# A new step order for a fused chunk-attention and phase-mixing kernel

## The chip, the cores and the metric

One Trainium2 chip, one core. The metric is the device time of one execution in microseconds; a kernel's time is the median over several runs.

## The reference

Attention inside chunks of 64 positions, then a token-mixing layer with phases, and a channel mixing with a relu. Eight batches, eight heads of 64 (so 512 channels), 576 positions, all in float32.

```python
# attention, for each batch, head and chunk of 64 positions
scores = (1 / sqrt(64)) * q_c @ k_c.T
attn = softmax(scores)                 # over the 64 keys of the chunk
x = attn @ v_c                         # heads side by side: [8, 576, 512]
# mixing
theta = x @ w_theta                    # 512 x 512
zr, zi = x * cos(theta), x * sin(theta)
y = w_tok_r @ zr + w_tok_i @ zi        # over the 576 positions
u = x + y
out = u + relu(u @ w_ch)               # 512 x 512
```

## The kernel before

**Tiles.** Two batches make a pair; there are four pairs, p = 0 to 3. A pair's 1152 positions are nine tiles of 128: tiles 0 to 3 are the first batch's, 5 to 8 the second's, and tile 4 holds the last 64 positions of each. For the attention part the tiles are taken in five groups: A (tiles 0, 1), B (2, 3), M (tile 4 alone), C (5, 6), D (7, 8). Everything is computed in fp16 with fp32 sums.

**Steps.** The whole kernel is a list of steps, written out in the string `ORDER`. A step is `kind.pg` or `kind.pg.slot`: the kind, the pair, the group or tile, and for steps that write PSUM the slot. There are three wide slots (two banks each) and two thin ones (one bank each); a step that writes a slot waits until the step that last used it has been read. The kinds are:

- on GpSimd (POOL), loads: `q`, `k`, `v` (two DMAs of 128 KB for a group, of 64 KB for M; L174, L182), `lw` the token weights in four parts (L192, L197), `lc` the channel weights (L200); `init` makes the identity matrix with a memset and a select on POOL.
- on TensorE (PE): `T` transposes q and k of a group (L262), `S` the scores (L308), `V0` and `V1` attention times v for the heads of either half (L341), `X` transposes x (L372), `H` (or `Ha`, `Hb` for a single tile) theta (L410), `Y` (or `Ya`, `Yb`, `Yc` in three parts) token mixing of one tile, 9 matmuls of 512 columns (18 narrower ones for tile 4; L480), `U` transposes u (L497), `W` channel mixing, 4 matmuls (L517), `TW` transposes the token weights (L236), `D` an idle matmul on a blank tile (L157).
- on VectorE (DVE): `tq` copies a T result from PSUM to SBUF (L285, L287), `v0` and `v1` divide by the softmax sum (L353, L354), `xv` copies an X result (L384), `z`, `za`, `zb` multiply x by cos and sin (L440 to L449), `y` adds x (L488), `uv` copies a U result (L511), `w` adds the relu and u (L526), `twd` copies a TW result (L247, L249).
- on ScalarE (ACT): `tqa`, `x` and `ua` do what `tq`, `xv` and `uv` do, `e` is the exponential (L321), `g`, `ga`, `gb` the cosine and sine (L426, L430[...]), `ct` casts w_theta once, `sa` issues half of a late tile's store.
- on SyncE (SP), in one queue: `Ud` and `Xd` transpose u or x of late tiles by DMA (L505, L393), `zm` moves half of the middle tile's z between partitions (L454, L455), `st` issues a tile's store, two DMAs, one for the last pair (L543), `lt` loads w_theta once.
- `new` only hands out a pair's tiles.

Each engine runs its own steps strictly in the order of the list; between engines, semaphores make a step wait for what it reads and for the buffers that it writes. A step late on one engine holds back all that stands behind it there.

**Buffers.** q and k of a group lie together in one of eight `qk` buffers, taken in turn at the group's first load, and given back by `T`. v has room for two pairs. x, zr and zi of a pair lie in one of two sets.

The string is read once, in this loop:

```python
with tc.manual_schedule():
    for step in ORDER:
        kind, at, *slot = step.split(".")
        g = int(at[1]) if at[1].isdigit() else at[1]
        work[kind](int(at[0]), g, *map(int, slot))
```

Of the kernel before, what the change touches and what calls it, by code (L numbers as in the profile page):

```python
# [15 lines left out]


ORDER = """
ones.00 D.00.0 lt.00 D.00.1 D.00.0 D.00.1 D.00.0 D.00.1 q.0M q.0B D.00.0 D.00.1 D.00.0
new.00 D.00.1 D.00.0 D.00.1 D.00.0 lw.00 D.00.1 q.0A D.00.0 D.00.1 k.0M lw.01 D.00.0  # L20
D.00.1 D.00.0 D.00.1 D.00.0 init.00 k.0B D.00.1 D.00.0 D.00.1 D.00.0 D.00.1 D.00.0
D.00.1 k.0A D.00.0 D.00.1 D.00.0 D.00.1 D.00.0 ct.00 D.00.1 D.00.0 D.00.1 TW.00.0 D.00.0
v.0M v.0A q.0C D.00.1 D.00.0 D.00.1 D.00.0 D.00.1 T.0M.1 tq.0M S.0M.2 e.0M TW.01.1
D.00.0 T.0B.2 twd.00 D.00.1 D.00.0 v.0B D.00.1 T.0A.0 D.00.0 q.0D lw.02 twd.01 D.00.1
V0.0M.1 tq.0A tqa.0B v0.0M S.0A.2 e.0A V1.0M.0 S.0B.1 v1.0M D.00.0 e.0B X.0M.2 V0.0A.0
k.0C V1.0A.1 x.0M H.0M.2 new.10 v0.0A v1.0A X.0A.0 xv.0A V1.0B.1 Ha.0A.1 v1.0B V0.0B.0
g.0M ga.0A v0.0B lw.03 k.0D z.0M Hb.0A.0 v.0C q.1C X.0B.1 TW.02.2 twd.02 gb.0A T.0C.0
x.0B q.1D Ha.0B.1 zm.0M Hb.0B.0 tq.0C zb.0A za.0A v.0D TW.03.1 ga.0B gb.0B S.0C.2 twd.03
q.1M T.0D.0 e.0C lc.00 Ya.02.1 zb.0B Ya.03.0 k.1D Yb.02 Yb.03 za.0B Yc.03 y.03 Yc.02
y.02 Ya.01.0 Yb.01 U.02.1 tqa.0D V1.0C.1 S.0D.2 q.1B e.0D V0.0C.0 Yc.01 ua.02 V1.0D.2  # L30
v1.0C v0.0C X.0C.1 V0.0D.0 Ya.00.1 y.01 Yb.00 k.1M xv.0C H.0C.1 Yc.00 v0.0D v1.0D y.00
v.1M X.0D.0 xv.0D T.1D.2 k.1C v.1D tq.1D g.0C U.03.0 U.00.1 k.1B ua.00 uv.03 H.0D.0
W.03.1 q.1A z.0C U.01.0 T.1M.1 g.0D w.03 st.03 S.1D.2 W.02.1 tq.1M S.1M.0 T.1C.1 ua.01
z.0D e.1D Y.06.0 w.02 tq.1C e.1M V0.1M.2 S.1C.1 T.1B.0 v.1C q.2C q.2M k.1A q.2D v0.1M
y.06 W.01.1 e.1C V1.1M.2 tq.1B V1.1D.1 v1.1M v.1B Y.04.0 q.3B w.01 V0.1C.0 st.02 v1.1D
S.1B.2 V0.1D.1 v0.1D k.2M e.1B Y.08.1 y.04 Y.07.0 v.1A k.2C X.1M.2 x.1M v0.1C T.1A.1
X.1D.0 V1.1C.2 y.08 U.04.1 ua.04 y.07 v1.1C st.01 tq.1A x.1D Y.05.0 V0.1B.2 X.1C.0
S.1A.1 e.1A x.1C y.05 W.04.1 U.06.0 v0.1B w.04 H.1M.2 W.00.1 q.2A uv.06 w.00 g.1M
V1.1B.1 v1.1B H.1C.0 z.1M H.1D.2 g.1C U.08.0 U.05.1 uv.08 V0.1A.1 V1.1A.0 v1.1A ua.05
v0.1A W.08.0 W.06.1 g.1D w.06 v.2M k.2D w.08 st.04 T.2C.0 st.00 z.1D X.1B.1 q.2B X.1A.2  # L40
x.1B v.2D W.05.1 x.1A H.1B.1 H.1A.2 v.2C w.05 tq.2C U.07.0 k.2A zm.1M g.1B z.1C Y.16.1
S.2C.0 st.06 v.2B ua.07 g.1A y.16 T.2D.1 T.2M.2 tq.2D new.20 k.2B U.16.0 Y.18.1 tq.2M
q.3D e.2C ua.16 y.18 z.1B S.2M.1 e.2M z.1A st.05 S.2D.0 T.2A.2 V0.2M.1 Y.15.0 y.15
tqa.2A W.16.1 e.2D V0.2C.2 v0.2M v0.2C v.3D V1.2C.0 k.3B q.3A w.16 v1.2C Y.13.0 S.2A.1
V1.2D.2 v.2A V0.2D.0 W.07.1 y.13 e.2A w.07 v1.2D v0.2D st.08 Y.10.0 U.15.1 st.16 V1.2M.1
v1.2M y.10 X.2C.2 T.2B.0 ua.15 Y.14.1 tq.2B q.3M x.2C X.2M.1 y.14 S.2B.2 X.2D.0 x.2M
e.2B Y.17.0 U.10.1 V0.2B.1 k.3A T.3A.2 v.3A v0.2B x.2D ua.10 q.3C T.3B.0 y.17 tqa.3B
W.15.1 w.15 k.3M H.2M.1 W.10.0 U.13.1 tq.3A uv.13 st.07 w.10 g.2M H.2C.0 V1.2B.2 V1.2A.1
st.10 g.2C W.13.1 U.18.0 ua.18 k.3D st.15 v1.2B z.2M w.13 st.13 H.2D.2 Y.12.0 g.2D
W.18.1 v1.2A T.3D.0 y.12 S.3B.1 z.2C T.3M.2 zm.2M k.3C w.18 z.2D Y.11.0 tq.3M v.3M e.3B  # L50
Y.27.1 S.3M.1 tqa.3D T.3C.2 y.11 S.3A.0 e.3M st.18 V0.2A.1 Y.28.0 tq.3C y.27 v0.2A e.3A
V0.3M.0 Xd.2A Ud.11 new.30 S.3D.2 v.3B V0.3B.1 e.3D v0.3M Ud.14 y.28 Xd.2B v0.3B v.3C
Y.25.1 V1.3M.0 V1.3A.2 S.3C.1 Ud.17 v1.3M Ud.27 Y.26.0 y.25 V0.3A.0 v1.3A e.3C V1.3C.1
v0.3A Xd.3A V1.3B.2 v1.3C W.14.1 w.14 y.26 H.2A.0 Xd.3M v1.3B W.11.1 H.2B.1 w.11 st.14
st.11 g.2A z.2A g.2B Ud.12 W.27.0 w.27 st.27 Ud.26 H.3A.2 g.3A W.17.1 Ud.25 z.2B w.17
st.17 H.3M.0 g.3M Xd.3B Y.24.0 y.24 V1.3D.1 Ud.24 V0.3D.2 V0.3C.0 v0.3D W.12.1 Ud.28
v1.3D w.12 Y.21.0 Y.22.1 st.12 v0.3C Xd.3D y.21 W.26.0 Ud.21 y.22 w.26 W.25.1 w.25
Y.23.0 y.23 st.26 st.25 H.3B.2 z.3A W.24.1 w.24 W.21.0 w.21 Xd.3C st.21 Ud.23 z.3M zm.3M
W.28.1 H.3D.1 Y.20.0 w.28 st.24 Ud.22 st.28 y.20 H.3C.0 g.3B z.3B W.23.1 g.3D w.23
Y.31.0 Y.32.1 y.31 W.22.0 st.23 g.3C Ud.20 z.3C y.32 Ud.31 w.22 Ud.32 Y.30.1 z.3D W.20.0  # L60
y.30 Y.38.1 w.20 st.20 y.38 st.22 W.31.0 Ud.38 w.31 Ud.30 Y.37.1 y.37 Y.35.0 y.35 W.32.1
w.32 W.38.0 Ud.35 sa.31 w.38 Y.33.1 W.30.0 y.33 st.38 sa.38 st.32 st.31 Y.36.1 sa.32
w.30 Y.34.0 y.36 sa.30 st.30 y.34 Ud.37 W.35.1 w.35 sa.35 Ud.33 W.33.0 w.33 sa.33 W.37.1
Ud.36 Ud.34 w.37 W.36.0 st.35 w.36 st.33 W.34.1 D.00.0 sa.37 st.37 D.00.0 D.00.0 st.36
w.34 D.00.1 D.00.0 sa.36 D.00.1 D.00.0 D.00.1 D.00.0 sa.34 D.00.1 D.00.0 st.34
""".split()


# [565 lines left out]
```

The softmax here doesn't subtract the row's maximum and nothing guards it: scores larger than these inputs give would overflow.

## Time and profile before

| | us |
|---|---|
| median of 9 runs (lowest to highest) | 203.41 (202.08 to 205.58) |
| the profiled execution, whole | 202.6 |
| the profiled execution, span from first to last instruction | 200.8 |
| PE busy, of it idle matmuls | 190.8, 17.1 |
| DVE, ACT, POOL busy | 127.8, 93.0, 106.1 |
| PE clock granted, over the span | 1.0 |
| last load issued by POOL, from the span's start | 115.3 |

All times inside the kernel are counted from the start of the span. The profile is of one execution, 0.8 us below the median. Busy time says how full an engine is, not what it waits for: the chain of work that ended last tells which engine or transfer set the time in a stretch, and a timeline gives each group of instructions with its start, its length, and in brackets the idle time before it and what ended that.

| stretch (us) | PE busy in it | idle matmuls in it | POOL |
|---|---|---|---|
| 0 to 11.7 | nearly all | 36 | loads from 1.24 on |
| 11.7 to 36.0 | work from the first transpose to tile 02's mixing | 13 | loads |
| 36.0 to 69.1 | all but 1.0 us | 0 | loads |
| 69.1 to 137 | all | 0 | loads until 115.3 |
| 137 to 196.1 | all but 2.0 us | 0 | idle |
| 196.1 to 200.8 | last store | 11 | idle |

### The profile page before, as it was taken

What the parts mean: (1) busy time and instruction counts of PE and PEld (TensorE: products, weight loads), DVE (VectorE), ACT (ScalarE), POOL (GpSimd) and SP (SyncE); (2) the same over time, 40 slices, a digit from 0 to 9 for tenths busy, and PEclk for the clock granted to TensorE, in tenths of its full rate; (3) what the DMA queues carried; (4) which work ended last, traced back from release to release, by engine and by line L of the source; (5) the groups of instructions that cost most, each with busy time, mean ns of one, the idle gap of its engine ahead of it and who ended that gap; (6) DMA issues with size and microseconds to landing.
All of it is one profiled execution on the core that took longest, in us unless ns stands there. A gap on an engine that the chain in (4) does not pass through costs nothing.

```text
span 200.8 us, 6347 instructions
## 1 busy us (share of the span) xinstructions
PE 190.8 (95%) x2766; PEld 95.1 (47%) x2766; DVE 127.8 (64%) x235; ACT 93.0 (46%) x100; POOL 106.1 (53%) x133
## 2 busy tenths in 40 slices
PE   7988789999999999999999999999999899999986
PEld 2434455545554645455465555543444344344432
DVE  0014689387885867948874786977684566844461
ACT  2304877556922488797247976427900444000000
POOL 7999999788998999987998800000000000000000
PEclk9999999999999999999999999999999999999999
DMA  5999999999999999999999992179777886683775
GB/s 191 170 169 155 159 186 167 153 176 145 168 191 186 155 166 213 180 207 170 163 208 153 144 229 64 32 145 117 152 123 148 176 168 131 134 171 64 216 167 163
DMA packets 140090, 32.01 MB, mean 159 GB/s; under 512 B 132768, under 2 KB 134944, under 8 KB 140064
## 3 DMA queue, kind: packets, MB, share of 16 engines
q0 software_dynamic: 114288, 16.02, 119.0%
q1 hardware_dynamic: 25056, 14.43, 31.2%
q10 hardware_dynamic: 720, 1.18, 2.0%
q8 instruction: 21, 0.34, 0.7%
q14 instruction: 5, 0.04, 0.1%
HBM read 33.06 MB, written 9.44 MB: 212 GB/s over the span
## 4 chain that ended last, share of the span: by engine, by line
PE 57%; DMA 21%; POOL 18%; issue 3%; DVE 0%; SPq 0%; POOLq 0%
PE ps_y L480 25%; PE ps_uw L517 12%; POOL qk L174 11%; PE ps_theta L410 10%; DMA v<-in_v_dram 7%; DMA uT<-u 5%; POOL v L182 5%; DMA qk<-in_q_dram 4%; DMA wch<-in_moe_w_ch_dram 3%; PE ps_qkT L262 2%; PE ps_x L341 2%; PE ps_sT L308 2%; DMA xT<-x 2%; POOL wnat L192 1%; PE ps_idle L157 1%
## 5 line engine op out<-in xcount | busy, mean ns | idle before, releaser
L480 PEld LDWEIGHTS <-wT 128*128 128x128 f16 (+1 forms) x360 | 30.8, 100 | 35.0 <-issue 1.2
L480 PE MATMUL ps_y<-zr,wT 128*128 128x512 f16 (+1 forms) x180 | 44.4, 381 | 0.0
L480 PE MATMUL ps_y<-zi,wT 128*128 128x512 f16 (+1 forms) x180 | 41.8, 379 | 0.0
L488 DVE TENSOR_TENSOR u<-ps_y,x 128x512 f16<-128x512 f32 x36 | 24.7, 687 | 24.8 <-PE ps_y L480 23.3
L517 PE MATMUL ps_uw<-wch,uT 128*128 128x512 f16 x144 | 36.4, 380 | 1.7 <-DMA uT<-u 1.7
L182 POOL DMA_DIRECT2D v<-in_v_dram x40 | 34.0, 870 | 3.4 <-DMA qk<-in_q_dram 1.1
L174 POOL DMA_DIRECT2D qk<-in_q_dram x40 | 34.1, 874 | 2.7 <-issue 1.0
L174 POOL DMA_DIRECT2D qk<-in_k_dram x40 | 34.2, 868 | 2.4 <-DMA v<-in_v_dram 0.8
L410 PE MATMUL ps_theta<-wtheta,xT 128*128 128x512 f16 x144 | 34.3, 380 | 0.5 <-DMA xT<-x 0.3
L426 ACT ACTIVATE cos<-ps_theta,pihalf 128x1024 f16<-128x1024 f32 (+1 forms) x22 | 21.1, 960 | 26.0 <-PE ps_theta L410 23.1
L321 ACT ACTIVATE eT<-ps_sT 128x1024 f16<-128x1024 f32 (+1 forms) x20 | 18.6, 938 | 28.2 <-PE ps_sT L308 28.2
L526 DVE SCALAR_TENSOR_TENSOR o<-ps_uw,u 128x512 f32<-128x512 f32 x36 | 24.7, 688 | 10.5 <-PE ps_uw L517 9.8
L354 DVE TENSOR_TENSOR x<-ps_x,recip 128x512 f16<-128x512 f32 (+1 forms) x40 | 25.5, 638 | 1.4
L517 PEld LDWEIGHTS <-uT 128*128 128x128 f16 x144 | 12.7, 97 | 18.5 <-DMA uT<-u 4.6
L410 PEld LDWEIGHTS <-xT 128*128 128x128 f16 x144 | 13.2, 98 | 16.4 <-DMA xT<-x 0.8
L430 ACT ACTIVATE sin<-ps_theta 128x1024 f16<-128x1024 f32 (+1 forms) x22 | 19.0, 864 | 0.0
L157 PE MATMUL ps_idle<-blank 128*128 128x512 f16 x60 | 17.1, 432 | 1.3 <-DVE pihalf L145 1.2
L287 DVE COPY qkT<-ps_qkT 128x2048 f16<-128x2048 f16 x11 | 13.4, 1216 | 4.5 <-PE ps_qkT L262 4.5
L353 DVE RECIPROCAL recip<-ps_x 128x8 f32<-128x8 f32 (+1 forms) x40 | 7.8, 196 | 10.6 <-PE ps_x L341 10.3
L341 PE MATMUL ps_x<-v,eT 64*64 64x65 f16 x576 | 11.9, 196 | 2.0 <-DMA v<-in_v_dram 1.6
L262 PE MATMUL ps_qkT<-id,qk 64*128 64x64 f16 x576 | 12.2, 191 | 1.2 <-DMA qk<-in_k_dram 1.2
L341 PEld LDWEIGHTS <-eT 64*64 64x64 f16 x576 | 8.2, 106 | 9.2 <-issue 5.1
(42 smaller groups left out, 137.9 us busy)
## 6 DMA issues: line engine op xcount, KB each, us to landing
out_dram<-o SPq DMA_DIRECT2D x63, 128.0 KB, 2.8
qk<-in_q_dram POOLq DMA_DIRECT2D x32, 128.0 KB, 6.6
qk<-in_k_dram POOLq DMA_DIRECT2D x32, 128.0 KB, 6.7
v<-in_v_dram POOLq DMA_DIRECT2D x32, 128.0 KB, 6.5
out_dram<-o ACTq DMA_DIRECT2D x9, 128.0 KB, 2.8
theta<-in_moe_w_theta_dram SPq DMA_DIRECT2D x1, 1024.0 KB, 5.6
wnat<-in_moe_w_tok_r_dram POOLq DMA_DIRECT2D x2, 288.0 KB, 6.1
wnat<-in_moe_w_tok_i_dram POOLq DMA_DIRECT2D x2, 288.0 KB, 6.4
```

Source lines behind the costliest of these rows:

```text
L157: nc.tensor.matmul(ps, blank[:, 0:P], blank, start=True, stop=True)
L174: nc.gpsimd.dma_start(nats[p, g][rows, which, r], (q, k)[which][b, :, t0 : t0 + n, :].rearrange("h s d -> s h d"),)
L182: nc.gpsimd.dma_start(v16[rows, slot + r, :, 0:D], v[b, :, t0 : t0 + n, :].rearrange("h s d -> s h d"),)
L341: nc.tensor.matmul(psv[half[r], to, h4, :], eT[rows, h % 2, r if n == 2 else 0, h // 2, :], v16[rows, slot + (r if n == 2 else 0), h, 0 : ...
L354: nc.vector.tensor_tensor(out=st[p]["x"][:, j0 : j0 + n, f * NE * D : (f + 1) * NE * D].rearrange("p c (h d) -> p c h d", h=NE), in0=psv[: ...
L410: nc.tensor.matmul(ps[:, j * DM : j * DM + DM], xT[:, (j + (t or 0)) * NDB + db, :], wtheta16[:, db, :], start=(db == 0), stop=(db == NDB ...
L426: nc.scalar.activation(out=cos[:, 0:n].rearrange("p a e -> p (a e)"), in_=pin, func=AF.Sin, bias=pihalf, scale=1.0,)
L430: nc.scalar.activation(out=sin[:, 0:n].rearrange("p a e -> p (a e)"), in_=pin, func=AF.Sin)
L480: nc.tensor.matmul(ps[rows], wT[:, kt, cols], z[:, jz, :], start=(kt == 0), stop=(kt == 2 * KT),)
L488: nc.vector.tensor_tensor(out=u, in0=st[p].pop(("ps_y", j))[:, 0:DM], in1=st[p]["x"][:, j], op=ALU.add)
L517: nc.tensor.matmul(ps, uT[:, db * P : db * P + P], wch16[:, db, :], start=(db == 0), stop=(db == NDB - 1),)
L526: nc.vector.scalar_tensor_tensor(out=o, in0=st[p].pop(("ps_uw", j)), scalar=0.0, in1=u, op0=ALU.max, op1=ALU.add)
```

## The change

Only the string `ORDER` changes. The 651 steps are permuted; every tile goes through the same computation with the same matmuls, loads and stores. Twenty-five copies out of PSUM change the engine (`tq` and `tqa`, `x` and `xv`, `ua` and `uv`), most PSUM slots are given anew, and idle matmuls are put in other places. Loads change places in POOL's queue, and the transposes and stores in SP's.

The old order's head and end, and the whole new order:

```diff
-ones.00 D.00.0 lt.00 D.00.1 D.00.0 D.00.1 D.00.0 D.00.1 q.0M q.0B D.00.0 D.00.1 D.00.0
-new.00 D.00.1 D.00.0 D.00.1 D.00.0 lw.00 D.00.1 q.0A D.00.0 D.00.1 k.0M lw.01 D.00.0
-D.00.1 D.00.0 D.00.1 D.00.0 init.00 k.0B D.00.1 D.00.0 D.00.1 D.00.0 D.00.1 D.00.0
-D.00.1 k.0A D.00.0 D.00.1 D.00.0 D.00.1 D.00.0 ct.00 D.00.1 D.00.0 D.00.1 TW.00.0 D.00.0
-v.0M v.0A q.0C D.00.1 D.00.0 D.00.1 D.00.0 D.00.1 T.0M.1 tq.0M S.0M.2 e.0M TW.01.1
-D.00.0 T.0B.2 twd.00 D.00.1 D.00.0 v.0B D.00.1 T.0A.0 D.00.0 q.0D lw.02 twd.01 D.00.1
-V0.0M.1 tq.0A tqa.0B v0.0M S.0A.2 e.0A V1.0M.0 S.0B.1 v1.0M D.00.0 e.0B X.0M.2 V0.0A.0
-k.0C V1.0A.1 x.0M H.0M.2 new.10 v0.0A v1.0A X.0A.0 xv.0A V1.0B.1 Ha.0A.1 v1.0B V0.0B.0
-g.0M ga.0A v0.0B lw.03 k.0D z.0M Hb.0A.0 v.0C q.1C X.0B.1 TW.02.2 twd.02 gb.0A T.0C.0
-x.0B q.1D Ha.0B.1 zm.0M Hb.0B.0 tq.0C zb.0A za.0A v.0D TW.03.1 ga.0B gb.0B S.0C.2 twd.03
-q.1M T.0D.0 e.0C lc.00 Ya.02.1 zb.0B Ya.03.0 k.1D Yb.02 Yb.03 za.0B Yc.03 y.03 Yc.02
-y.02 Ya.01.0 Yb.01 U.02.1 tqa.0D V1.0C.1 S.0D.2 q.1B e.0D V0.0C.0 Yc.01 ua.02 V1.0D.2
-v1.0C v0.0C X.0C.1 V0.0D.0 Ya.00.1 y.01 Yb.00 k.1M xv.0C H.0C.1 Yc.00 v0.0D v1.0D y.00
-v.1M X.0D.0 xv.0D T.1D.2 k.1C v.1D tq.1D g.0C U.03.0 U.00.1 k.1B ua.00 uv.03 H.0D.0
-W.03.1 q.1A z.0C U.01.0 T.1M.1 g.0D w.03 st.03 S.1D.2 W.02.1 tq.1M S.1M.0 T.1C.1 ua.01
-z.0D e.1D Y.06.0 w.02 tq.1C e.1M V0.1M.2 S.1C.1 T.1B.0 v.1C q.2C q.2M k.1A q.2D v0.1M
-y.06 W.01.1 e.1C V1.1M.2 tq.1B V1.1D.1 v1.1M v.1B Y.04.0 q.3B w.01 V0.1C.0 st.02 v1.1D
...
-st.11 g.2A z.2A g.2B Ud.12 W.27.0 w.27 st.27 Ud.26 H.3A.2 g.3A W.17.1 Ud.25 z.2B w.17
-st.17 H.3M.0 g.3M Xd.3B Y.24.0 y.24 V1.3D.1 Ud.24 V0.3D.2 V0.3C.0 v0.3D W.12.1 Ud.28
-v1.3D w.12 Y.21.0 Y.22.1 st.12 v0.3C Xd.3D y.21 W.26.0 Ud.21 y.22 w.26 W.25.1 w.25
-Y.23.0 y.23 st.26 st.25 H.3B.2 z.3A W.24.1 w.24 W.21.0 w.21 Xd.3C st.21 Ud.23 z.3M zm.3M
-W.28.1 H.3D.1 Y.20.0 w.28 st.24 Ud.22 st.28 y.20 H.3C.0 g.3B z.3B W.23.1 g.3D w.23
-Y.31.0 Y.32.1 y.31 W.22.0 st.23 g.3C Ud.20 z.3C y.32 Ud.31 w.22 Ud.32 Y.30.1 z.3D W.20.0
-y.30 Y.38.1 w.20 st.20 y.38 st.22 W.31.0 Ud.38 w.31 Ud.30 Y.37.1 y.37 Y.35.0 y.35 W.32.1
-w.32 W.38.0 Ud.35 sa.31 w.38 Y.33.1 W.30.0 y.33 st.38 sa.38 st.32 st.31 Y.36.1 sa.32
-w.30 Y.34.0 y.36 sa.30 st.30 y.34 Ud.37 W.35.1 w.35 sa.35 Ud.33 W.33.0 w.33 sa.33 W.37.1
-Ud.36 Ud.34 w.37 W.36.0 st.35 w.36 st.33 W.34.1 D.00.0 sa.37 st.37 D.00.0 D.00.0 st.36
-w.34 D.00.1 D.00.0 sa.36 D.00.1 D.00.0 D.00.1 D.00.0 sa.34 D.00.1 D.00.0 st.34
+ones.00 D.00.0 lt.00 D.00.1 D.00.0 D.00.1 D.00.0 q.0M D.00.1 D.00.0 D.00.1 q.0B D.00.0
+D.00.1 lw.00 D.00.0 D.00.1 D.00.0 D.00.1 D.00.0 D.00.1 init.00 D.00.0 D.00.1 D.00.0
+D.00.1 D.00.0 D.00.1 D.00.0 D.00.1 q.0A D.00.0 D.00.1 D.00.0 D.00.1 TW.00.0 D.00.0
+D.00.1 twd.00 D.00.0 D.00.1 D.00.0 ct.00 k.0M D.00.1 T.0M.1 lw.01 k.0B tq.0M D.00.0
+D.00.1 D.00.0 S.0M.2 e.0M v.0M TW.01.0 D.00.1 D.00.0 T.0B.1 D.00.1 D.00.0 D.00.1 k.0A
+v.0A tqa.0B new.00 D.00.0 q.0D twd.01 T.0A.0 V1.0M.2 S.0B.1 D.00.1 D.00.0 v.0B D.00.1
+D.00.0 tqa.0A q.0C V0.0M.0 e.0B v1.0M lw.02 S.0A.2 D.00.1 v0.0M e.0A X.0M.1 V1.0A.0
+v1.0A x.0M lw.03 k.0D V0.0A.2 D.00.0 v0.0A k.0C H.0M.1 X.0A.0 V0.0B.2 q.1M xv.0A v0.0B
+g.0M Ha.0A.1 Hb.0A.0 V1.0B.0 v.0C gb.0A ga.0A z.0M TW.02.1 q.1D v1.0B twd.02 X.0B.2
+xv.0B lc.00 TW.03.0 zb.0A za.0A Hb.0B.0 gb.0B Ha.0B.1 ga.0B twd.03 T.0C.1 tq.0C v.0D
+q.1C Ya.02.0 Yb.02 Ya.03.1 Yb.03 za.0B zm.0M S.0C.2 e.0C q.1B k.1D zb.0B T.0D.0 tq.0D
+k.1M Yc.03 Yc.02 y.03 V1.0C.1 V0.0C.0 y.02 Ya.01.1 Yb.01 v.1M U.03.0 ua.03 v1.0C Yc.01
+v.1D k.1C y.01 W.03.0 w.03 S.0D.2 Ya.00.1 v0.0C e.0D U.02.0 X.0C.1 V1.0D.0 xv.0C v1.0D
+V0.0D.2 v0.0D Yb.00 Yc.00 q.1A k.1B H.0C.1 q.2C y.00 q.2M uv.02 k.1A X.0D.0 st.03 xv.0D
+T.1D.2 U.01.1 v.1C v.1A tq.1D g.0C H.0D.0 q.3C uv.01 g.0D z.0C T.1M.2 W.01.0 w.01 st.01
+W.02.1 v.1B T.1C.1 q.2A S.1D.0 tqa.1M z.0D S.1M.2 Y.06.0 w.02 U.00.1 e.1D k.2M V0.1D.0
+tq.1C T.1B.1 e.1M tqa.1B y.06 new.10 V1.1D.2 Y.04.0 V0.1M.1 v0.1D V1.1M.0 v1.1D ua.00
+q.2D S.1C.2 v1.1M q.3M q.3A y.04 Y.08.1 k.2C v0.1M U.04.0 y.08 uv.04 e.1C X.1M.0 X.1D.2
+x.1M T.1A.1 V0.1C.0 Y.07.1 tqa.1A xv.1D U.08.0 v0.1C V1.1C.2 uv.08 S.1A.0 v1.1C e.1A
+q.2B S.1B.1 W.04.0 y.07 H.1M.2 U.06.1 w.04 e.1B W.08.0 st.02 uv.06 Y.05.1 k.3A w.08 g.1M
+X.1C.0 V0.1B.1 V1.1B.2 y.05 U.07.0 v0.1B x.1C W.00.1 w.00 k.2A z.1M ua.07 H.1D.0 v1.1B
+U.05.0 g.1D uv.05 H.1C.1 g.1C new.20 V1.1A.2 V0.1A.0 k.2D W.06.1 v0.1A W.05.0 X.1B.0
+v1.1A X.1A.1 w.06 v.2M st.04 xv.1A w.05 x.1B v.2C k.2B T.2C.2 W.07.1 z.1C st.08 tqa.2C
+st.00 H.1B.1 w.07 z.1D H.1A.0 zm.1M Y.16.0 g.1B y.16 v.2D T.2M.2 z.1B S.2C.1 g.1A T.2D.0
+st.05 tqa.2M U.16.1 ua.16 Y.18.0 Y.15.1 e.2C tq.2D S.2D.2 y.18 S.2M.0 z.1A V1.2C.1
+W.16.0 y.15 U.15.1 st.07 v1.2C e.2D w.16 V0.2C.2 uv.15 T.2A.1 v.2B e.2M V1.2M.0 U.18.0
+v1.2M Y.13.1 T.2B.0 ua.18 v.3M tq.2A v0.2C tqa.2B V0.2M.1 q.3D y.13 X.2C.2 q.3B Y.10.0
+xv.2C S.2B.2 v0.2M V1.2D.1 v.2A k.3B S.2A.0 st.06 Y.14.1 e.2B V0.2D.2 e.2A v1.2D st.16
+y.10 V0.2B.1 X.2M.0 v0.2D x.2M W.18.0 y.14 H.2M.0 v0.2B Y.17.1 w.18 U.10.0 uv.10 g.2M
+H.2C.2 y.17 z.2M st.18 U.13.0 Y.12.1 ua.13 V1.2B.1 v1.2B T.3B.0 g.2C T.3A.2 zm.2M tqa.3B
+y.12 X.2D.1 k.3M v.3B xv.2D W.13.0 H.2D.1 z.2C W.10.1 T.3M.0 w.13 tqa.3A w.10 g.2D v.3A
+V1.2A.2 W.15.0 Y.11.1 v1.2A V0.2A.1 S.3B.2 z.2D w.15 st.15 st.13 y.11 k.3D st.10 Ud.17
+Ud.14 v0.2A tqa.3M T.3D.0 e.3B Y.25.0 tq.3D Ud.12 S.3A.1 Ud.11 k.3C T.3C.0 V0.3B.2 y.25
+tq.3C e.3A new.30 v0.3B Xd.2B Y.28.1 V1.3B.1 y.28 V0.3A.0 v0.3A S.3C.2 e.3C Y.27.0 v1.3B
+y.27 S.3M.0 V1.3A.2 e.3M S.3D.1 v.3C W.17.1 W.12.0 V0.3M.0 v1.3A Xd.2A Ud.27 Xd.3A e.3D
+V0.3C.2 V1.3M.1 w.17 v1.3M W.14.1 st.17 w.12 H.2B.1 g.2B v0.3C v0.3M W.11.0 w.11 H.2A.2
+Ud.28 W.27.0 w.14 Y.26.1 st.12 H.3A.0 st.11 Xd.3B g.2A Ud.25 st.14 w.27 z.2B g.3A st.27
+z.2A Xd.3M Y.24.0 v.3D y.26 V1.3D.1 y.24 V1.3C.2 V0.3D.0 Y.22.1 v1.3C y.22 W.28.0 Ud.24
+Ud.22 w.28 W.25.1 st.28 v0.3D H.3M.2 Xd.3C g.3M z.3A Y.20.0 Ud.26 w.25 y.20 Ud.20 v1.3D
+Y.23.1 H.3B.0 g.3B W.26.0 st.25 z.3M zm.3M y.23 w.26 st.26 W.24.1 Xd.3D w.24 W.20.0 w.20
+W.22.1 H.3C.2 z.3B st.24 Y.32.0 w.22 Y.21.1 st.22 st.20 g.3C Ud.23 y.32 Y.30.0 z.3C
+Ud.32 y.30 H.3D.1 g.3D y.21 Y.31.0 y.31 W.23.1 w.23 Ud.30 W.30.0 w.30 Ud.21 Ud.31 st.30
+Y.33.1 W.32.0 st.23 z.3D y.33 W.31.1 w.32 w.31 Y.38.0 st.31 Y.35.1 sa.30 sa.32 y.38
+Ud.38 st.32 y.35 Ud.35 W.21.0 w.21 sa.31 Y.37.1 y.37 W.38.0 Y.36.1 w.38 st.21 Ud.33
+Y.34.0 y.36 W.35.1 st.38 Ud.37 Ud.36 sa.38 y.34 W.37.0 w.35 w.37 Ud.34 W.33.1 w.33 st.35
+st.37 W.36.0 w.36 W.34.1 D.00.0 D.00.0 sa.35 sa.33 st.33 w.34 D.00.1 D.00.0 sa.36 D.00.1
+D.00.0 sa.37 D.00.1 D.00.0 st.36 D.00.1 st.34 D.00.0 sa.34 D.00.1
```

More of the change, by code (lines that the diff above doesn't have):

```diff
@@ L31 @@
-v1.0C v0.0C X.0C.1 V0.0D.0 Ya.00.1 y.01 Yb.00 k.1M xv.0C H.0C.1 Yc.00 v0.0D v1.0D y.00
-v.1M X.0D.0 xv.0D T.1D.2 k.1C v.1D tq.1D g.0C U.03.0 U.00.1 k.1B ua.00 uv.03 H.0D.0
-W.03.1 q.1A z.0C U.01.0 T.1M.1 g.0D w.03 st.03 S.1D.2 W.02.1 tq.1M S.1M.0 T.1C.1 ua.01
-z.0D e.1D Y.06.0 w.02 tq.1C e.1M V0.1M.2 S.1C.1 T.1B.0 v.1C q.2C q.2M k.1A q.2D v0.1M
-y.06 W.01.1 e.1C V1.1M.2 tq.1B V1.1D.1 v1.1M v.1B Y.04.0 q.3B w.01 V0.1C.0 st.02 v1.1D
-S.1B.2 V0.1D.1 v0.1D k.2M e.1B Y.08.1 y.04 Y.07.0 v.1A k.2C X.1M.2 x.1M v0.1C T.1A.1
@@ L37 @@
[L37 to L54, printed above, removed]
```

## The prediction

> **What bounds the kernel now.** I read the page's busy row first, then the chain that ended last, then the timelines of PE, ACT, DVE and SP.
>
> ```profile
> span 200.8 us, 6347 instructions
> PE 190.8 (95%) x2766; PEld 95.1 (47%) x2766; DVE 127.8 (64%) x235; ACT 93.0 (46%) x100; POOL 106.1 (53%) x133
> ```
>
> PE is busy 95% of the span, but 17.1 us of its 190.8 are the 60 idle matmuls (L157), so some 174 us are work. The rest of the span is where an order can gain: a head until work flows, gaps, and a tail. The chain says which feeder holds PE back:
>
> ```profile
> 28.87 7.25 DMA v<-in_v_dram
> ...
> 37.28 7.01 DMA wch<-in_moe_w_ch_dram
> ...
> 55.57 7.27 DMA qk<-in_q_dram
> ...
> 63.13 5.92 DMA v<-in_v_dram
> 69.05 0.04 issue
> 69.09 0.32 PE ps_x L341 x14
> ```
>
> Columns: start, duration, what. Up to 69.05 the chain is POOL's loads; after it, PE nearly alone. The PE timeline (start, duration, group, in brackets the idle before it and its releaser) gives the marks that I compare with:
>
> ```profile
> 1.19 10.61 PE L157 MATMUL ps_idle<-blank 128*128 128x512 f16 x36 [1.19 <-DVE pihalf L145]
> 11.73 0.64 PE L236 MATMUL ps_wT<-id,wnat 128*64 128x128 f16 x16
> ...
> 13.70 0.41 PE L262 MATMUL ps_qkT<-id,qk 64*128 64x64 f16 x16
> ...
> 18.54 0.38 PE L262 MATMUL ps_qkT<-id,qk 64*128 64x64 f16 x14 [0.50 <-DMA qk<-in_k_dram]
> ...
> 23.22 1.04 PE L410 MATMUL ps_theta<-wtheta,xT 128*128 128x512 f16 x4 [0.16 <-ACT xT L384]
> ...
> 36.02 0.59 PE L480 MATMUL ps_y<-zr,wT 128*128 128x512 f16 x2
> ...
> 60.54 0.32 PE L341 MATMUL ps_x<-v,eT 64*64 64x65 f16 x14 [0.56 <-DMA v<-in_v_dram]
> ...
> 140.65 1.90 PE L410 MATMUL ps_theta<-wtheta,xT 128*128 128x512 f16 x8 [0.28 <-DMA xT<-x]
> ...
> 159.02 1.90 PE L517 MATMUL ps_uw<-wch,uT 128*128 128x512 f16 x8 [0.98 <-DMA uT<-u]
> ...
> 195.11 1.04 PE L517 MATMUL ps_uw<-wch,uT 128*128 128x512 f16 x4 [0.43 <-DMA uT<-u]
> ```
>
> These are T.0M at 13.70, T.0A's k half at 18.54, H.0M at 23.22, Yc.03 at 36.02. From 36 to 69.1 PE idles 1.0 us (0.22 and 0.56 and 0.22 for v loads); from there to 137 nothing; after it 2.0 (0.28, 0.98, 0.16, some 0.2 at 191.8, 0.43). The late waits are SP's queue: it issues DMA transposes of 1.2 to 1.35 us and stores of about 0.6 in order, and is full from 148 to 160, so Ud.21 (issued 156.50) is late for W.21 at 159.02.
>
> ```profile
> 153.82 1.18 SPq L543 DMA_DIRECT2D out_dram<-o  x2
> 155.06 1.35 SPq L393 DMA_TRANSPOSE xT<-x  x1
> 156.50 1.21 SPq L505 DMA_TRANSPOSE uT<-u  x1
> ```
>
> **What the Trainium skill says.** "DMA: Bandwidth & Descriptors", section on the anatomy of one DMA on the gpsimd path, gives 2.0 us plus bytes over 436 GB/s, 2.3 us for 128 KB. The trace has about 6 us from a load's issue to its landing, up to 7.5 later; I use the trace. The same page, on why small descriptors are slow, charges 27% to 256 B pieces; the head pieces here are 64 floats, 132768 of 140090 packets are under 512 B, and the core moves 150 to 190 GB/s. That agrees in direction: a shuffled load order does not load faster. "VectorE: DVE Perf Modes", perf-mode tier table, caps copies from PSUM at 2x; "ScalarE: Activation LUTs", on what ACT_TABLE_LOAD costs, prices an ACTIVATE at 186 ns plus 0.833 per element. For a 2048 wide copy that is 1.89 us on ACT; the trace has 1863 ns on ACT and 1216 on DVE.
>
> **The change part by part.** The ORDER string has 651 steps before and after. The matmuls, loads and stores are the same; the 60 idle matmuls too (36 ahead of TW.00, 13 strewn, 11 last, against 28, 21 and 11). Counting runs of small matmuls (T, S, V, X) between wide ones from Yc.03 on gives 27 in both, so I price PE's work as unchanged.
>
> *Copies that change engine.* Nine tq become tqa and three go back; five x become xv; six ua become uv and two go back. DVE: -3x1.22 - 3x0.68 + 5x0.69 + 4x0.42 = -0.6 us. ACT: +3x1.86 + 3x1.01 (nearest row: ACT's 128x1024 copy) - 5x1.01 - 4x0.58 = +1.2. Neither is full, so as sums these are free (-0.3 to +0.5); what counts is where one is waited for.
>
> *POOL's head.* Before: q.0M, q.0B, lw.00, q.0A, k.0M, lw.01, init, k.0B, k.0A, v.0M, v.0A. After: init moves ahead of q.0A (memset and select, 0.62 us), v.0M ahead of k.0A (1.33 us). So k.0M and lw.01 land 0.62 later, k.0B unchanged, and k.0A's second issue goes from 12.2 to 13.5, landing 19.85 instead of 18.5. T.0M goes to 14.3, S.0M to 15.5, TW.01 to 15.8, T.0B to 16.95. TW.00's eight idle matmuls less (0.22 each) win nothing: T.0M is next and waits for k.0M.
>
> *The chain behind T.0A.* Its k half runs 19.85 to 20.25. The copy is now ACT's: 20.3 to 22.15 (before DVE, 1.23). Queued behind it on ACT are e.0B (to 23.1), e.0A (to 24.05) and x.0M (to 24.65). So V1.0A starts at 24.1, H.0M at 24.75 (+1.5), and on DVE v1.0A and v0.0A end at 26.15; X.0A follows (+1.95), xv.0A, Ha.0A at 27.4 (+1.9). Then DVE is full: v0.0B to 28.1, z.0M (four halves, 1.8) to 29.9, v1.0B 30.7, twd.02 31.5, xv.0B 32.15, za and zb of 0A 33.5, twd.03 34.5, tq.0C 35.9, za and zb of 0B 37.3. Yc.03 needs these: **37.6 against 36.02, +1.6**, with the same matmuls done.
>
> *37 to 69.* PE's sums, plus the waits I can place: X.0C behind w.03 and v0.0C on DVE 0.6; S.1M behind g.0D on ACT 0.15; T.1B on k.1B (second issue about 52.1, 6 us) 0.35; V0.1C on v.1C, which POOL now issues four pairs of loads later (about 58.7, +6.8) 0.6. That puts S.1A at 68.3. The matmuls left then, at 1.94 a Y, 0.87 a W, 1.73 an H, 0.57 T, 0.38 S, 0.25 V, 0.34 X, 0.22 U, are 2.2 us more than before had left at 69.1: **lag 1.4**. The ring of eight qk buffers costs nothing: q.3C takes 0C's buffer at about 62, T.0C ended near 35; if T were late there, POOL would stall by as much.
>
> *69 to 137.* Before idles nowhere. After has four hand-offs with almost no room: X.1A needs g.1C's PSUM, T.2D needs g.1A's, H.2M comes 0.87 behind X.2M, H.2D the same behind X.2D (a copy and its wait take 0.8 to 0.95). Estimate 0.8 for these together; 0 to 1.6.
>
> *137 to the end.* I added up SP's queue from Y.25 on with its own durations. Xd.3A is issued 10 us after Y.25's start and needed at 19; Ud.30 lands 1.3 ahead of W.30, Ud.31 about 1.2 ahead of W.31, zm.3M 1.5 ahead of Y.32's last matmul. Only Ud.34 stays: y.34, then the transpose, land up to 0.6 behind the four W that cover it (before: 1.0, SP being 0.5 late). So 2.0 of idle become about 0.5: **-1.5**. What is late next is again W.34. The stores behind it (2.8 us to landing) are as before.
>
> **Sum:** +1.4 + 0.8 - 1.5 = +0.7 us on the span of 200.8. The profiled execution took 202.6, so it would be 203.3; the median of nine runs is 203.41, 0.8 above it, so 204.1.
>
> **The rivals.** 0.3% is 0.6 us, about what a measurement of this kernel can tell from no change.
> (1) *SP's late queue decides, the head doesn't* (ends faster). If the lag at S.1A is 0.7, because v.1C lands a microsecond sooner and DVE finds a gap in the head, and the middle loses nothing, then 0.7 - 1.9 = -1.2: 202.2. It decides once the lag is under 0.9. For it: the late waits are in the trace and go; the loads from k.1M to v.1A get more room than before on paper. Against: DVE's head sum has no hole of 0.7.
> (2) *The terms cancel*: middle near 0, +1.4 - 1.5: 203.3. For it: four hand-offs are tight, none is clearly short.
> (3) *The loads bite deeper*: v.1C lands 8.2 us after its issue instead of 6.8, as loads do around 83 us in this trace; POOL, which keeps about eight loads in flight, then stalls with it, and V0.1C with all PE work queued behind it: lag 1.4 + 1.4 = 2.8, and 2.8 + 0.8 - 1.5 gives 205.5. Against: landings between 46 and 64 us took 4.2 to 7.3.
> (4) The string does not set the engines' order: unlikely, since PE's timeline follows it step by step; it would give 203.4.
>
> **How the numbers follow.** Forecast (slower, 204.1; its own range 203.9 to 205.0) 0.34; (1) 0.36; (2) with (4) 0.20; (3) 0.10. So faster 0.36, same 0.20, slower 0.44. Leaving out a tenth at each end, the range is 201.8 to 205.8: the low end is the head lag at 0.5 and a gain of 2.1, the high end (3).
>
> **What would show it.** In the new profile T.0A's second half should start near 19.9, H.0M near 24.8, Yc.03 near 37.6; the gaps at 140 and 159 should be gone. If Yc.03 is below 37 or S.1A below 67.6, the head step is wrong and rival (1) stands; if PE idles over 1 us between 69 and 137 or for uT after 140, the last two steps are.

## The result and the profile after

The changed order takes 206.0 us in the median (204.43 to 208.11), the order before 203.42 beside it; the ratio is 1.0137, with a 95% interval from 1.0114 to 1.016. It is slower by 1.4%, 2.6 us: 1.9 more than forecast and 0.2 above the range. (The medians here and below are over all executions; the ratios leave out those that took over 1.5% longer than the fastest of the same kernel.) The profiled execution took 206.02 us with a span of 204.2, 3.4 above the span of before; 0.8 of the 3.4 comes from the profile of before, which lies that much below its median, while this one lies at its own.

From the page of the changed kernel, its busy row and the granted clock in 40 slices (a digit is the clock in tenths of full speed, 9 for 0.9 and more):

```profile
span 204.2 us, 6331 instructions
PE 192.0 (94%) x2766; PEld 95.6 (47%) x2766; DVE 126.5 (62%) x238; ACT 94.5 (46%) x97; POOL 106.1 (52%) x133
...
PEclk9999699999999999999999999999999999999999
```

PE is busy 1.2 us longer with as many matmuls, most of it in the one stretch with a slow clock: from 20 to 25.5 us it is busy 4.90 us, and 4.05 in the trial below with two transposes moved, which has the same head and a full clock there. It also stands idle 2.2 us longer. The PE timeline (start, duration, group, idle before it and releaser) has the marks that the prediction named:

```profile
20.07 0.53 PE L262 MATMUL ps_qkT<-id,qk 64*128 64x64 f16 x14 [1.32 <-DMA qk<-in_k_dram]
...
25.62 1.03 PE L410 MATMUL ps_theta<-wtheta,xT 128*128 128x512 f16 x4
...
38.60 0.60 PE L480 MATMUL ps_y<-zr,wT 128*128 128x512 f16 x2
...
68.47 0.72 PE L308 MATMUL ps_sT<-qkT 64*64 64x64 f16 x64
...
90.73 0.38 PE L262 MATMUL ps_qkT<-id,qk 64*128 64x64 f16 x14 [0.28 <-DMA qk<-in_k_dram]
...
135.14 1.04 PE L517 MATMUL ps_uw<-wch,uT 128*128 128x512 f16 x4 [0.60 <-DMA uT<-u]
...
139.14 1.90 PE L410 MATMUL ps_theta<-wtheta,xT 128*128 128x512 f16 x8 [1.49 <-DMA xT<-x]
...
155.39 1.04 PE L410 MATMUL ps_theta<-wtheta,xT 128*128 128x512 f16 x4 [0.80 <-DMA xT<-x]
```

These are T.0A's k half, H.0M, Yc.03, S.1A (with S.1B), T.2D, then W.12, H.2B and H.3M. The first four stand where the prediction put them, or up to 1 us later. The gaps of before at 140 and 159 are gone, as forecast, but the last three lines show three others in their place, 2.89 us together. The timeline of SP's queue (start, duration, what) shows why:

```profile
112.61 0.48 SPq L454 DMA_DIRECT2D zr<-zmid  x1
113.21 0.54 SPq L455 DMA_DIRECT2D zi<-zmid  x1
123.73 4.78 SPq L543 DMA_DIRECT2D out_dram<-o  x6
128.62 6.52 SPq L505 DMA_TRANSPOSE uT<-u  x4
135.19 3.19 SPq L393 DMA_TRANSPOSE xT<-x  x2
```

SP issues nothing from 113.75 to 123.73, and then is full. What ends its idleness is w.15 on DVE (PE ended W.15 at 121.89, but DVE had z.2D ahead of w.15):

```profile
123.02 0.68 DVE L526 SCALAR_TENSOR_TENSOR o<-ps_uw,u 128x512 f32<-128x512 f32 x1
```

The next step in SP's queue is st.15, and behind it stand st.13 and st.10, whose w ended at 119.30 and 121.05, then Ud.17, whose u was ready since about 112. The six store issues take 4.78 us and the four transposes 6.52, so Xd.2B, which H.2B needs, is issued at 135.19.

### The profile page after: what moved, and what is told of

It reads as the page before. It is cut to its first block, busy times and chain, and to the rows that moved or that the text cites. A ratio compares the mean times of both kernels' runs of the same rounds, so it can differ in the third digit from the quotient of the medians.

```text
span 204.2 us, 6331 instructions
## 1 busy us (share of the span) xinstructions
PE 192.0 (94%) x2766; PEld 95.6 (47%) x2766; DVE 126.5 (62%) x238; ACT 94.5 (46%) x97; POOL 106.1 (52%) x133
## 4 chain that ended last, share of the span: by engine, by line
PE 71%; POOL 10%; DMA 10%; DVE 5%; issue 1%; ACT 1%; SPq 0%; POOLq 0%
PE ps_y L480 34%; PE ps_uw L517 12%; PE ps_theta L410 11%; POOL qk L174 9%; DMA qk<-in_k_dram 7%; PE ps_qkT L262 4%; PE ps_x L341 3%; DMA xT<-x 3%; PE ps_sT L308 2%; DVE x L354 2%; PE ps_idle L157 2%; PE ps_uT L497 1%; PE ps_xT L372 1%; POOL wnat L192 1%; DVE o L526 1%
## 5 line engine op out<-in xcount | busy, mean ns | idle before, releaser
L517 PE MATMUL ps_uw<-wch,uT 128*128 128x512 f16 x144 | 35.7, 380 | 0.6 <-DMA uT<-u 0.6
L354 DVE TENSOR_TENSOR x<-ps_x,recip 128x512 f16<-128x512 f32 (+1 forms) x40 | 25.5, 638 | 1.4
L157 PE MATMUL ps_idle<-blank 128*128 128x512 f16 x60 | 18.3, 448 | 1.4 <-DVE pihalf L145 1.2
L287 ACT COPY qkT<-ps_qkT 128x2048 f16<-128x2048 f16 x8 | 14.8, 1867 | 6.5 <-PE ps_qkT L262 6.4
L262 PE MATMUL ps_qkT<-id,qk 64*128 64x64 f16 x576 | 12.9, 192 | 2.6 <-DMA qk<-in_k_dram 2.5
L262 PEld LDWEIGHTS <-qk 64*128 64x128 f16 x576 | 10.0, 95 | 7.4 <-DMA qk<-in_k_dram 3.7
L441 DVE TENSOR_TENSOR zi<-x,sin 128x1024 f16<-128x1024 f16 (+1 forms) x18 | 11.2, 624 | 0.0
```

Of the source, the lines that this page charges most:

```text
L157: nc.tensor.matmul(ps, blank[:, 0:P], blank, start=True, stop=True)
L262: nc.tensor.transpose(psv[:, r, w, e, j, :], t[half[r], w, j, 2 * e : 2 * e + 2, :].rearrange("s h d -> s (h d)"), id16[half[r], half[r]],)
L354: nc.vector.tensor_tensor(out=st[p]["x"][:, j0 : j0 + n, f * NE * D : (f + 1) * NE * D].rearrange("p c (h d) -> p c h d", h=NE), in0=psv[: ...
L517: nc.tensor.matmul(ps, uT[:, db * P : db * P + P], wch16[:, db, :], start=(db == 0), stop=(db == NDB - 1),)
```

## The experiments

The loss can be split in more than one way. Three theories: **head and SP queue** (the head costs what the trace shows at S.1A, about 1.6 us, SP's queue the rest); **loads pace everything to 69 us**, so that the head's own chain does not matter; **SP's load in all**, and not its order, bounds the late stage. Each time is the median, each ratio is to the order before, timed beside it on the same chip.

**Old head on the new order.** The steps ahead of T.1D in the changed order, put in the order, on the engines and in the slots of before (in short; steps are matched by kind, pair and group, whatever their engine and slot):

```diff
-order = after
+order = [s for s in before if s in after[:i]] + after[i:]     # i: T.1D (first trial), Yc.03 (second)
```

> The changed order, but all its steps ahead of T.1D (about the first 50 us) stand in the order, on the engines and in the slots of the order before. Theory 'head and SP queue': the head costs what the trace shows at S.1A, about 1.6 us, and the rest of the loss lies after 134 us; so about 204.4, that is 1.0 us above before. Rival 'loads pace everything to 69 us': the head's lag would be made anyway by the loads that follow, 205.7 to 206.0, as the changed kernel. Rival 'all of it is the head': 203.4.

> The changed order with the old head again, but cut ahead of Yc.03 (about 37 us) and not ahead of T.1D, since the seam of the first trial made W.03 wait 1.05 us for its uT. Theory 'the head costs about 0.8 us, as the new head in the old order did, and the rest of the changed order costs the remaining 1.8': 205.2. Rival 'the rest of the changed order is paced by its own loads up to 66 us, so a sooner head is lost again': 205.8 to 206.1, with new gaps for k.1B and v.1C between 55 and 67 us.

206.17 us, 1.0156 (1.0102 to 1.0211), and 208.22, 1.0269 (1.0215 to 1.0324), six executions each. The first is near the rival's number; no theory had the second. Its PE timeline has the reason:

```profile
44.66 1.87 PE L517 MATMUL ps_uw<-wch,uT 128*128 128x512 f16 x4 [3.08 <-DMA wch<-in_moe_w_ch_dram]
```

The new order runs W.03 early and so loads the channel weights early (lc behind q.1D); behind the old head's loads they come too late. In the second trial PE's granted clock then fell too, to 0.66 in the mean from 42 to 52 us. In the first trial W.03 waited 1.05 us and a U behind it 0.21, at the seam. So neither trial prices the head. They show that the new order hangs on its own load order. The late gaps were there in both (in the first, 1.96 us for xT at 140).

**New head on the old order.**

```diff
-order = before
+order = [s for s in after if s in before[:i]] + before[i:]    # i: T.1D
```

> The mirror of the run with the old head: the order before, with its steps ahead of T.1D put in the changed order. Theory 'head and SP queue': 203.4 + 1.6 = 205.0, with the gaps for uT and xT after 137 us as in the kernel before. Rival 'loads pace everything': 203.4 to 203.8. If this loss and that of the rest don't add up to the 2.6 us of the whole change, the two halves interact.

204.26 us, 1.0039 (1.0013 to 1.0065): 0.8 us, 0.3 to 1.3 by the interval. Its groups H.1B and H.1A, one line of the timeline, start here:

```profile
82.69 3.63 PE L410 MATMUL ps_theta<-wtheta,xT 128*128 128x512 f16 x16
```

In the profile of before they start at 81.49. That is not a lag of 1.2 us for sure: two other profiles with the old head, of the trials below that alter only the late part of the order before, have them at 81.88 and 82.80. The waits for loads between 36 and 69 us, 1.0 in the profile of before, are gone here; one of 0.41 for u on DVE is in their place. By the medians the head costs about a third of the change's loss, and by the interval at most half.

**Two transposes of x ahead of the stores.**

```diff
-w.15 st.15 st.13 y.11 k.3D st.10 Ud.17 Ud.14 v0.2A ... y.25 Xd.2B ... Xd.2A Ud.27
+w.15 Xd.2B st.15 st.13 y.11 k.3D st.10 Ud.17 Ud.14 v0.2A Xd.2A ... y.25 ... Ud.27
```

> The changed order with two steps moved in SP's queue: Xd.2B ahead of st.15, st.13 and st.10, and Xd.2A right behind v0.2A, so ahead of Ud.12 and Ud.11. Theory 'SP queue': the PE gaps of 0.60 us (W, for uT) and 1.49 us (H.2B, for xT) between 134 and 139 us go, less up to 0.5 that comes back at the next wait on SP: 204.0 to 204.5. Rival 'the transposes are late because their x is late, or PE pays elsewhere': 205.6 to 206.0.

205.82 us, 1.0129 (1.0075 to 1.0183), six executions: no gain that can be measured. The wait for xT is gone, but W now waits for its uT, longer than both gaps together:

```profile
136.68 1.04 PE L517 MATMUL ps_uw<-wch,uT 128*128 128x512 f16 x4 [2.67 <-DMA uT<-u]
```

So it is not which transpose goes first: at 134 us all of them were late.

**The same in the order before.**

```diff
-st.12 v0.3C Xd.3D y.21 W.26.0 Ud.21
+v0.3C y.21 Ud.21 st.12 Xd.3D W.26.0
```

> The order before with three late steps moved: y.21 and Ud.21 ahead of st.12 and Xd.3D, so that Ud.21 is issued some 2.7 us sooner. Theory 'SP queue': the 0.98 us gap ahead of W.21 at 158 us goes; up to 0.3 may come back where Xd.3D and the stores are now later: 202.4 to 202.8. Rival 'the late stage is bound by what the queue has to do in all, not by its order': the gap moves to the next W or H, 203.4.

203.22 us, 0.9995 (0.9968 to 1.0021): no change. The gap of 0.98 us at 159 is gone, and one of 0.58 stands at 171.42, for uT too. Here the full queue handed most of its gap on.

**Stores and a transpose moved into SP's idle stretch.**

```diff
-w.13 tqa.3A w.10 g.2D ... w.15 st.15 st.13 y.11 k.3D st.10 Ud.17 Ud.14
+w.13 Ud.17 st.13 tqa.3A w.10 st.10 g.2D ... w.15 st.15 y.11 k.3D Ud.14
```

> The changed order with three steps moved up in SP's queue, to where SP stands idle from 114 to 124 us: Ud.17 and st.13 right behind w.13, st.10 right behind w.10. They stood behind st.15, which waits for w.15. Theory 'SP's backlog': four stores and one transpose, 4.5 us of issue, are out of the way when w.15 ends at 123.7, so the W for uT and H.2B find their tiles: the 2.09 us of gaps between 134 and 139 go, 0 to 0.8 comes back later: 204.0 to 204.8. Rival 'the transposes themselves are slow there (1.3 to 2.5 us each), whatever precedes them': at least 1.2 of the gap stays, 205.2 or more.

202.43 us, 0.9964 (0.9939 to 0.9988): **faster than both kernels**, 3.6 us below the changed order, a larger gain than either theory had. SP's queue now:

```profile
112.66 1.41 SPq L505 DMA_TRANSPOSE uT<-u  x1
118.14 5.52 SPq L543 DMA_DIRECT2D out_dram<-o  x6
123.76 5.33 SPq L505 DMA_TRANSPOSE uT<-u  x3
129.14 3.44 SPq L393 DMA_TRANSPOSE xT<-x  x2
```

Xd.2B goes out at 129.14, 6 us sooner, and from 45 us to the end PE's timeline has a single gap:

```profile
173.63 1.04 PE L517 MATMUL ps_uw<-wch,uT 128*128 128x512 f16 x4 [0.46 <-DMA uT<-u]
```

**One step alone.**

```diff
-w.15 st.15 st.13 y.11 k.3D st.10 Ud.17 Ud.14
+w.15 st.13 y.11 k.3D st.10 Ud.17 st.15 Ud.14
```

> The changed order with one step moved: st.15 behind Ud.17 and not ahead of st.13. Theory 'head-of-line block': st.15 waits for w.15 until 123.7 and holds back stores and a transpose that were ready; with it last of the four the kernel is as the one with three steps moved up, 202.3 to 203.0. Rival 'the gain of that kernel came from issuing Ud.17 already at 112, well ahead of its place': most of the loss stays, 204.5 or more.

202.62 us, 0.9976 (0.9952 to 1.0). With st.15 last of the four, SP is at work from 119.31, when w.13 has ended, and not from 123.73:

```profile
119.31 2.85 SPq L543 DMA_DIRECT2D out_dram<-o  x4
122.27 1.31 SPq L505 DMA_TRANSPOSE uT<-u  x1
123.71 1.13 SPq L543 DMA_DIRECT2D out_dram<-o  x2
124.95 4.55 SPq L505 DMA_TRANSPOSE uT<-u  x3
129.55 3.53 SPq L393 DMA_TRANSPOSE xT<-x  x2
```

One step, moved behind three others in one queue, takes away the whole of what the change cost. The rival, that Ud.17 at 112 us made the gain, is out: here Ud.17 is issued at 122.27. That is a head-of-line block: the first of a queue waits, and what is ready behind it waits with it.

**Half of the late stores on ACT**, in either order:

```diff
-"st": store(p, j, (nc.sync, nc.sync if p < 3 else None))
+"st": store(p, j, (nc.sync, None if p == 3 else nc.scalar if (p, j) in ON_ACT else nc.sync))
```

> The changed order, with the second half of the stores of tiles 11, 12, 14, 17 and 20 to 28 issued by ACT and not by SP, at the same places. Theory 'what SP has to do in all bounds the late stage': 13 issues of 0.6 us leave SP from 134 us on, so the gap of 0.80 at 155 goes; the gaps at 134 to 139 stay for the most part, since the stores of 15, 13 and 10 stay on SP: 205.0 to 205.4. Rival 'the order on SP counts, not its load': 205.8 to 206.2. Rival 'ACT's stores hold back its sines behind a w': 206.4 or more.

> The order before, with the same thirteen half stores on ACT. Theory 'what SP has to do in all bounds the late stage': the gaps for uT and xT at 140, 159 and 174 us (1.42 us together) go: 202.0 to 202.4. Rival 'the order counts': as the kernel before, 203.2 to 203.6, as the run with Ud.21 moved ahead was.

In the changed order 205.84 us, 1.0053 (1.002 to 1.0085). The two numbers do not agree: the median is hardly below 206.0, and the ratio rests on 11 of the 22 executions. In the order before 203.3 us, 0.9987 (0.9961 to 1.0012). (Lines count one more in these kernels.) The changed order has its wait behind st.15 still, since that block lies before the thirteen moved issues. The gaps at 135 and 155 are gone, one of 0.59 for uT comes at 176, and that at 139 is longer:

```profile
138.35 1.90 PE L411 MATMUL ps_theta<-wtheta,xT 128*128 128x512 f16 x8 [1.99 <-DMA xT<-x]
```

The gain is between 0.1 and 0.8%, so whether SP's load counts beside its order is not settled by this trial. In the order before no gain is to be measured: the wait of 0.98 for uT is gone, but others of 0.63 for uT and 0.35 for ACT's sine come, and in the profiled execution the loads of v at 62 us held PE back by 1.02.

**The tail, and T.0A's chain**, on top of the three moved steps:

```diff
-sa.36 D.00.1 D.00.0 sa.37          # tail
+sa.37 sa.36 D.00.1 D.00.0
-tqa.0A                             # second trial: and the copy on DVE
+tq.0A
-v.0M k.0A                          # third trial: and the load order of before
+k.0A v.0M
```

> The changed order with Ud.17, st.13 and st.10 moved up (202.43 when timed alone), and with sa.37 ahead of sa.36 on ACT. In the profiles of the changed order the span ends 4.5 us after w.34, before 3.9, since ACT issues sa.36, sa.37 and sa.34 one behind the other after w.36. Theory 'ACT's last three stores': 0.5 to 0.6 us less than that kernel: 201.8 to 202.0. Rival 'the tail is the landing of the last store on SP': no change, 202.3 to 202.6.

> The kernel of the tail trial with T.0A's copy on DVE, which stands idle from 16 to 20 us, in place of ACT. Theory 'the head's lag comes through ACT's copy': S.0A and with it H.0M, X.0A and the chain on DVE start 0.8 to 1.0 us sooner; k.1B and v.1C land no sooner, so 0.3 to 0.6 of it reaches the end: 201.3 to 201.7. Rival 'loads pace the first 66 us': no change against the tail trial, new gaps for DMA between 55 and 67 us.

> As the trial with T.0A's copy on DVE, and k.0A's load ahead of v.0M's as in the order before. Theory 'the load order of the head costs': T.0A's k half at 18.5 and not 19.5 to 20.5, 1.3 us less lag at H.0M than the changed order has, in all 0.3 to 0.8 less than with the copy alone: 200.8 to 201.4. Rival 'loads pace the first 66 us': no change against that trial.

Each trial keeps the steps of the one ahead of it. 202.94 us, 0.9986 (0.9963 to 1.0008); 202.47, 0.9958 (0.9936 to 0.998); 202.22, 0.9956 (0.9922 to 0.9989). The tail's swap brings nothing that can be measured. In its profile the span ends 4.25 us after w.34 and not 4.5, but the kernel with st.15 alone moved, without the swap, has 4.4. The intervals of all three overlap, none reached the gain expected of it, and the steps are not told apart by time. The trace shows more. In the third trial the head is nearly that of before:

```profile
18.21 0.38 PE L262 MATMUL ps_qkT<-id,qk 64*128 64x64 f16 x14 [0.21 <-DMA qk<-in_k_dram]
...
23.84 1.03 PE L410 MATMUL ps_theta<-wtheta,xT 128*128 128x512 f16 x4
...
34.80 0.38 PE L262 MATMUL ps_qkT<-id,qk 64*128 64x64 f16 x14 [1.01 <-DMA qk<-in_k_dram]
...
55.63 0.38 PE L262 MATMUL ps_qkT<-id,qk 64*128 64x64 f16 x14 [0.55 <-DMA qk<-in_k_dram]
...
74.16 0.41 PE L372 MATMUL ps_xT<-id,x 64*128 64x64 f16 x16
```

H.0M comes at 23.84, where the tail trial has 25.67, but T.0C waits 1.01 us for k.0C and T.1B 0.55 for k.1B, and X.1C is where it was (74.16, and 74.22 in the tail trial). One profile is not much to go by here: six kernels (the changed order and five trials that alter it from 112 us on) have one and the same head, and their profiles have H.0M at 24.31 to 25.67, S.1A at 67.57 to 68.73 and X.1C at 73.08 to 74.24. The third trial's H.0M lies ahead of them all, and its X.1C at their late end. What the head wins is lost again before 74 us, and the two waits in between that the other kernels do not have are for loads. No trial moved k.0C or k.1B, so that the load order takes it back is read from the trace and not shown.

## Why the prediction was wrong, point by point

- **Slower, and why at the head: right in size, in part by luck.** T.0A was put at 19.85 and came at 20.07, H.0M at 24.75 and came at 25.62, Yc.03 at 37.6 and came at 38.60, S.1A at 68.3 and came at 68.47. With 2.2 us more work left, that is a lag (the time by which PE is behind the order before, at the same work left) of 1.6 against 1.4 forecast. But two errors cancel in it: Yc.03 came 1.0 us late, and of the waits forecast behind it, 1.7 us, only that of X.0C was there (0.46 for 0.6). The lag also differs between executions: the six profiles with this head give 0.7 to 1.8. The sum of the chain from T.0A to H.0M, 4.9 us, was right: three profiles with the changed head and a full clock have 4.8, and the 5.55 of this one hold the slow clock. T.0M, put at 14.3, ran from 12.40 on, which did not count, since T.0A waits for its load. That the chain through ACT's copy is what makes the lag at 69 us is not borne out: with that copy on DVE and k.0A first, H.0M is sooner and X.1C is not. The waits in that trial speak for the new order of the loads, k.0C and k.1B. k.1B and v.1C made no gap in the changed kernel itself; PE may have come late enough.
- **Copies that change engine, free as sums: not contradicted.** DVE went from 127.8 to 126.5 us of busy time, ACT from 93.0 to 94.5; -0.6 and +1.2 were forecast.
- **69 to 137, four tight hand-offs at 0.8: wrong in place.** None of them made a gap. T.2D waited 0.28 us for its load of k. The two gaps of this change at 134 to 139 stand at the stretch's end and belong to the next point.
- **137 to the end, -1.5: the step that failed.** It "added up SP's queue from Y.25 on with its own durations" and names nothing that the queue still had to do at that moment. Y.25 started at 124.85. SP had then just begun on six store issues and had four transposes of u ahead of Xd.2B, since st.15 had held the queue from 113.75 on. So Xd.2B was issued 10.3 us after Y.25's start, at 135.19, and Xd.3A, which the prediction put at 10 us after it, at 139.81, 15.0 after it. The four Ud took 1.63 us each and not 1.2 to 1.35. The late gaps became 2.9 us in place of 0.5; before has 2.0. With st.15 alone moved, Xd.2B is issued 4.7 us after Y.25's start and Xd.3A 10.1: the sum was right for a queue that nothing has held up. A gap of 0.47 was left after 137 (0.46 with three steps moved), and 0.5 was forecast; that is luck, since it stands ahead of W.30, which was given 1.3 us to spare, and W.34, which was to wait, did not.
- **The tail, no change: off by 0.6.** The span ends 4.5 us after w.34, before 3.9. ACT issues its half of tile 34's store, sa.34, 0.6 us after w.34's end and before at once, because sa.36 and sa.37 go out just ahead of it, one behind the other. With the two swapped it is 0.6 still. No trial moved one of them away.
- **The sum.** 1.6 at S.1A, 0.3 at T.2D, 0.9 in the late gaps and 0.6 in the tail are 3.4, the difference of the spans. The forecast had 1.4, 0.8, -1.5 and 0. Most of the error, 2.4, is the late term.
- **The rivals.** (3), the loads that bite deeper, came nearest with 205.5, but its mechanism, V0.1C waiting for v.1C, did not occur. (1), which ends at 202.2 because SP's waits go, has the number of the kernel without st.15's block, 202.43 and 202.62; it set the late gain at 1.9 where the sum has 1.5, without a reason, and its lag of 0.7 is in the first of the two profiles, while the second has 1.8.
- **The signs.** None of the signs of being wrong would have told: Yc.03 and S.1A lie on the forecast's side, the gaps at 140 and 159 are gone, PE idles 0.9 us from 69 to 137, and after 140 it waits for xT and not for uT. They were set where the old gaps lay, and the largest new one lies between, at 137.6 to 139.1.

The order before does not have the block, and its SP queue shows what a sum from Y.25 on takes for granted:

```profile
121.26 1.45 SPq L543 DMA_DIRECT2D out_dram<-o  x2
128.53 1.34 SPq L393 DMA_TRANSPOSE xT<-x  x1
```

There SP stands idle from 122.71 to 128.53, just ahead of its late transposes, so a sum may begin there with an empty queue. In the changed order the sum had to begin where SP last stood idle, which is at st.15, with the time of w.15.

## What to carry to other kernels

SP's queue issues its DMAs in order, so a store put ahead of transposes was not free: it waited for its data and held what was ready behind it. Here one store, moved behind three steps that were ready sooner, was worth 1.6% of the kernel. When such a queue is summed up for a new order, begin where the queue last stands empty, carry each step's own ready time, and look for idle time of the queue with ready work behind its head. Where the queue was full instead, moving transposes ahead (two trials) took their gaps away and left one elsewhere, without a gain in time.

## What the runs showed that I had not expected

- PE's granted clock fell in the changed order's profile (0.66 of full speed in the mean from 20 to 25 us; four idle matmuls in a row took 1.89 us there, and 1.04 in the kernel with three steps moved). In the 5 us from 15 to 20 PE had been busy 3.05 us, and its longest idle time was 1.32. What brings this about is open: two other profiles with the changed head had less work there (2.9 and 2.7 us busy in the 5 us up to 20.5 and 20.3) and longer idle times (1.78 and 1.64), and kept the full clock. From T.0A's k half to H.0M the slow clock cost about 0.75 us (5.55 for 4.8). The time of the whole does not show it: the executions of the changed kernel with a mean clock under 1 (10 of 17) and those without have one median, 206.0 us.
- SP's DMA transposes of one tile are not of one length. Behind the six stores those at 130 to 134 us took 1.19 to 2.48 us to issue, and two of them 3.7 and 4.3 us to landing, where 2.5 is usual in this queue. The stores are not needed for it: the order before has one of 1.97 us at 135.28, landing after 3.8, with no store for 12 us ahead of it. What stretches them was not tried.
